# Attention and a softplus MLP on one core: the first stretch of all five engine queues written out as lists

## The chip, the cores and the metric

One of the eight cores of a Trainium2 chip. The core has five engines with a queue of their own, each strictly in order: TensorE (PE, matrix products), VectorE (DVE), ScalarE (ACT), GpSimd (POOL) and SyncE (SP, here the issuer of DMAs). Engines wait for each other through semaphores. The metric is the device time of one execution in microseconds, the median of several runs; lower is better.

## The reference

```python
q_d = q.reshape(B, H, Sd, factor, D).mean(axis=3)      # B, H, S, D = 4, 8, 576, 64; factor 4
...                                                    # k_d, v_d the same way
out_d = sm_attn(q_d, k_d, v_d)                         # softmax attention on 144 rows
out_up = np.repeat(out_d, factor, axis=2)
mask = np.abs(pos[:, None] - pos[None, :]) < factor
scores = np.where(mask, scale * np.matmul(q, k.transpose(0, 1, 3, 2)), -1000000000.0)
...                                                    # softmax of scores
out = out_up + np.matmul(attn, v)
x = out.transpose(0, 2, 1, 3).reshape(B * S, H * D)    # 2304 x 512
h = x @ w_in                                           # 512 x 2048
g = np.maximum(h, 0.0) + np.log1p(np.exp(-np.abs(h)))
return g @ w_out                                       # 2048 x 512
```

Inputs and outputs are float32.

## The kernel before

Attention runs in 16 units: unit u is one batch and one pair of heads (units 0 to 3 are batch 0). The MLP runs over 5 groups of 512 tokens (the last is shorter) and, within a group, over 16 tiles of 128 hidden features. A layer-1 tile h is 12 products of 128x512, a layer-2 tile adds 12 more into four accumulators acc. Each factor is split into a high part rounded to what TensorE reads (`fp32r`) and a low remainder, and three of the four products of parts are taken. The layer-1 input x of group 0 is batch 0's attention output, so the first layer-1 tiles need units 0 to 3.

One unit's steps, with the names that the lists of the change use for them (`name.unit`) and the engine that did them in batch 0 before:

- loads on SP: `q`, `k` (tiles qT, kT, already transposed), `vr` (v in rows, tile stage), `vw` (v in windows)
- `qd`, `kd`: sums of four neighbours (DVE); `block`: two scaled copies of qd (ACT); `vd`: the same sums of v, two additions (POOL)
- `psd`: downsampled scores (PE); `mxd` maximum (DVE), `expd` (ACT), `smd` reciprocal of the sum (DVE), `normd` (POOL); `pt0`, `pt1` transposes (PE, tile pdt), `sdT0`, `sdT1` copies (ACT)
- `psc`: local scores as 48 small products (PE), with the mask added by a product of the identity; `mx`, `sub` (DVE), `exp` (ACT), `sum`, `sm` (DVE), `norm` (POOL), `sT` transpose (DVE). Later units have the mask added on DVE (`mask`) in place of that product
- `po`: 4 + 48 products with vd and vw (PE), `od` (ACT), `x` two additions (DVE), `xh` rounded (ACT), `xl` remainder (POOL)

A weight block (`i` for layer 1, `o` for layer 2, `.f` for the tile) is loaded as 64-bit numbers and narrowed: `load` (SP), `top` (ACT), `or` (DVE), `hi` (ACT), `lo` (DVE). Layer-1 tile i: `l1_c.i` are the parts of its 12 products (tiles 0 to 2 in four quarters c of three products), then `abs`, `expln` (ACT), `max` (DVE), `gh` (POOL), `gl` (DVE), and `l2.i` the 12 products of layer 2. `fill_xh`, `fill_xl` are the part of batch 0 that belongs to group 1.

The order of all instructions is a planner's. `Plan.order` goes through time with a cost in microseconds for each operation: an engine that is free takes, of those whose inputs are ready and whose buffers can be had, the one of lowest priority number. Priorities are set by hand (batch 0's units start at `B0`, the others at `BS`). Delays are `LAT` = 0.2 between engines and `PE_LAT` = 0.8 or a `gap` in front of TensorE's steps; DMA runs at `DMA_RATE` = 0.33 MB/us with `DMA_LAT` = 2.0. `Plan.warm` then puts fillers into each gap that the plan has on TensorE ahead of layer 1: `busy(n)` issues n products of the identity with the mask (128x384) into a bank that nobody reads. A fixed 8 small ones (128x128) stand first:

```python
busy(8, identb)
for o in plan.warm(plan.order(), busy):
    o.fn()
```

The plan's order is what the engines get; the semaphores are added from the data that each instruction reads and writes.

Of the kernel before, what the change touches and what calls it, by code (L numbers as in the profile page):

```python
# [25 lines left out]
P = 128  # L26
# [27 lines left out]
TOP_POOL = lambda which, f: False  # L54
V_PE = ()
WL_POOL = lambda which, f: False
GL_ENG = lambda g: "DVE"
V_POOL = (0,)
NORM0 = "POOL"
O_POS = 4  # L60
NSPLIT = 3
BLOCK0 = "ACT"
KD_POOL = ()
XL_POOL = (0,)
# [39 lines left out]
class Plan:  # L104
    LAT = 0.2
    PE_LAT = 0.8
# [3 lines left out]
    DMA_LAT = 2.0  # L110
    DMA_RATE = 0.33
    AHEAD = 8
    def __init__(self, caps):
        self.caps, self.ops, self.state = caps, [], {}

    def op(self, eng, cost, prio, fn, r=(), w=(), after=(), kb=0.0, lat=None, block=False, port=False):
        o = Op(eng, cost, prio, fn)
        o.kb, o.block, o.port = kb, block, port or eng == "POOL"
        o.lat = lat if lat is not None else self.PE_LAT if eng == "PE" else self.LAT
# [22 lines left out]
    def order(self):  # L142
        waiting = {}
        line = {}
        for i, o in enumerate(self.ops):
# [8 lines left out]
        free = {e: 0.0 for e in waiting}  # L154
        port = 0.0
        frees = []
        dma_free, pos = 0.0, -50
# [3 lines left out]
        def ready_at(o):  # L161
            x = 0.0
            for d in o.deps:
                if d.end is None:
                    return None
                if d.eng == o.eng and d.eng != "SP":
                    x = max(x, d.end)
                else:
                    x = max(x, d.end + o.lat)
            return x  # L170

        while done < len(self.ops):
# [4 lines left out]
            for e, pend in waiting.items():  # L177
# [3 lines left out]
                for o in pend:  # L181
                    if o.prio > max(pos, 0 if e != "SP" else pos) + (self.AHEAD if pos >= 0 or e != "SP" else self.FETCH):
                        continue
# [15 lines left out]
                    if not turn:  # L199
# [41 lines left out]

    def warm(self, out, fill):
        last, extra = None, []
        for o in [x for x in out if x.eng == "PE"]:
            if last is not None:
                n = int((o.start - last) / self.FILL)
                if n > 1:
                    n += 2
                if n > 0:
                    x = Op("PE", 0.0, 0, lambda n=n: fill(n))  # L250
                    x.start = last
                    extra.append(x)
            if o.prio >= 0:
                break
            last = o.start + o.cost
        return sorted(out + extra, key=lambda o: o.start)
# [3 lines left out]
def kernel(  # L260
# [69 lines left out]
    def load(bf, src, prio, kb):  # L330
        return op("SP", 0.35, prio, lambda: nc.sync.dma_start(out=bf.t, in_=src), w=[bf], kb=kb)
# [3 lines left out]
    def attention(u, s):  # L335
# [3 lines left out]
        gap = 0.3 if early else 0.8  # L339
# [20 lines left out]
        if u in ON_PE:  # L360
# [11 lines left out]
            op("PE", 4.0, sS - 0.5, mm_sums, r=[q, k], w=[sums], lat=gap)  # L372
            qsum, qr = (lambda: sums.t[:, :SD]), [sums]
            op("ACT", 0.31, sS - 0.2, lambda: nc.scalar.copy(kd.t, sums.t[:, SD : 2 * SD]), r=[sums], w=[kd])
        else:
            qsum, qr = (lambda: qd.t), [qd]
            for dst, src, kk in ((qd, q, slice(0, S)), (kd, k, slice(REACH, REACH + S))):
                if src is k and u in KD_POOL:
                    ks = buf("ks", [P, 2, SD], 1, f"ks{u}", F32, first)

                    def pool_k(src=src, kk=kk, ks=ks):
                        v = src.t[:, kk].rearrange("c (s f) -> c f s", f=FACTOR)
                        nc.gpsimd.tensor_tensor(out=ks.t, in0=v[:, 0:2], in1=v[:, 2:4], op=ALU.add)
# [12 lines left out]
                    r=[src], w=[dst],  # L396
                )

        def copies():
            for j in range(2):  # L400
                hp = slice(j * D, (j + 1) * D)
                if be == "POOL":
                    nc.gpsimd.tensor_scalar(
                        out=bl[hp, j], in0=qsum()[hp], scalar1=scale, scalar2=None, op0=ALU.mult
                    )
                else:
                    nc.scalar.activation(out=bl[hp, j], in_=qsum()[hp], func=AF.Copy, scale=scale)

        be = BLOCK0 if early else "ACT"
        op(be, 0.66, sS - 1.5, copies, r=qr, w=[blk])  # L410
# [536 lines left out]
```

## Time and profile before

| what | us |
|---|---|
| median of 3 runs | 500.35 |
| lowest, highest | 500.2, 503.07 |
| profiled execution, its own time | 502.2 |
| profiled execution, span of the trace | 500.4 |
| TensorE busy in the span | 489.1 |
| VectorE busy | 269.3 |
| ScalarE busy | 245.0 |
| GpSimd busy | 92.6 |
| DMA, share of the 16 engines in queue q1 | 26.4% |

The profile is of one execution; the span lies between its first and its last recorded instruction. An engine's busy time is the union of its instructions' spans. Neighbours overlap a little, so the step from one row's start to the next row's start, and not a row's own duration, is what an instruction takes of its queue.

### The profile page before, as it was taken

How to read it: one execution, taken by the hardware profiler on the slowest of the kernel's cores; microseconds unless marked ns; L12 is line 12 of the kernel's file. 1: busy time of each engine (PE TensorE's matmuls, PEld its weight loads, DVE VectorE, ACT ScalarE, POOL GpSimd, SP SyncE). 2: the span in 40 equal slices, each digit the busy share in tenths (PEclk: the TensorE clock that was granted, in tenths of full speed). 3: DMA queues.
4: the chain of work that ended last, by engine and by line, in shares of the span. 5: the costliest groups of instructions: out<-in, count | busy, mean ns of one | idle time of the engine just before them, and what ended most of it. 6: DMA issues, size and time to landing. Idle time of an engine off the chain costs nothing.

```text
span 500.4 us, 12503 instructions
## 1 busy us (share of the span) xinstructions
PE 489.1 (98%) x5388; PEld 407.0 (81%) x5388; DVE 269.3 (54%) x512; ACT 245.0 (49%) x528; POOL 92.6 (19%) x133
## 2 busy tenths in 40 slices
PE   6999999999999999999999999999999999999996
PEld 4668778888878888888888888888888888889996
DVE  5668998898878646374274636453332222223322
ACT  3457988678656435434354535343442332334442
POOL 5633231131111121020011201120011001010110
PEclk9989999999999999999999999999999999999999
DMA  8924576666724303030114111100020000002001
GB/s 275 343 56 150 188 221 220 213 182 203 203 61 138 101 2 105 3 104 18 39 50 140 49 56 50 33 3 1 0 85 0 1 1 0 1 0 86 1 1 42
DMA packets 15798, 42.86 MB, mean 86 GB/s; under 512 B 1792, under 2 KB 2304, under 8 KB 15744
## 3 DMA queue, kind: packets, MB, share of 16 engines
q1 hardware_dynamic: 15600, 41.94, 26.4%
q8 instruction: 42, 0.69, 0.6%
q14 instruction: 12, 0.10, 0.1%
q10 hardware_dynamic: 144, 0.13, 0.1%
HBM read 37.35 MB, written 4.72 MB: 84 GB/s over the span
## 4 chain that ended last, share of the span: by engine, by line
PE 96%; DVE 1%; ACT 1%; DMA 1%; issue 0%
PE acc L809 40%; PE h L744 39%; PE po L593 5%; PE psc L492 3%; PE busy L900 3%; PE psd L429 3%; PE po L585 2%; PE pdt L561 2%; DMA qT<-in_qt_dram 1%; DVE qd L392 0%; DVE kd L392 0%; DVE wo0l L723 0%; PE psc L485 0%; DVE t L773 0%; DVE wri L698 0%
## 5 line engine op out<-in xcount | busy, mean ns | idle before, releaser
L773 DVE SCALAR_TENSOR_TENSOR t<-h,t 128x512 f32<-128x512 f32 (+1 forms) x80 | 50.7, 634 | 136.9 <-ACT t L768 136.9
L764 ACT ACTIVATE t<-h 128x512 f32<-128x512 f32 (+1 forms) x80 | 44.3, 554 | 156.7 <-PE h L744 151.9
L782 POOL TENSOR_SCALAR gh<-t 128x512 fp32r<-128x512 f32 (+1 forms) x80 | 51.6, 646 | 339.3 <-PE acc L809 152.4
L790 DVE TENSOR_TENSOR gl<-t,gh 128x512 fp32r<-128x512 f32 (+1 forms) x80 | 52.4, 655 | 40.7 <-POOL gh L782 40.7
L744 PE MATMUL h<-xh,wi0h 128*128 128x512 f32 (+1 forms) x160 | 60.7, 380 | 0.7 <-DVE t L773 0.7
L809 PE MATMUL acc<-gh,wo0h 128*128 128x512 f32 (+1 forms) x160 | 59.8, 374 | 0.0
L809 PE MATMUL acc<-gh,wo1h 128*128 128x512 f32 (+1 forms) x160 | 59.6, 373 | 0.0
L744 PE MATMUL h<-xh,wi1h 128*128 128x512 f32 (+1 forms) x160 | 59.5, 372 | 0.0
L809 PE MATMUL acc<-gl,wo1h 128*128 128x512 f32 (+1 forms) x160 | 59.1, 369 | 0.0
L744 PE MATMUL h<-xh,wi0l 128*128 128x512 f32 (+1 forms) x160 | 59.0, 369 | 0.0
L744 PE MATMUL h<-xl,wi0h 128*128 128x512 f32 (+1 forms) x160 | 59.0, 369 | 0.0
L809 PE MATMUL acc<-gl,wo0h 128*128 128x512 f32 (+1 forms) x160 | 58.9, 368 | 0.0
L744 PE MATMUL h<-xh,wi1l 128*128 128x512 f32 (+1 forms) x160 | 58.8, 368 | 0.0
L809 PE MATMUL acc<-gh,wo1l 128*128 128x512 f32 (+1 forms) x160 | 58.8, 368 | 0.0
L809 PE MATMUL acc<-gh,wo0l 128*128 128x512 f32 (+1 forms) x160 | 58.8, 368 | 0.0
L744 PE MATMUL h<-xl,wi1h 128*128 128x512 f32 (+1 forms) x160 | 58.8, 368 | 0.0
L768 ACT ACTIVATE t<-t 128x512 f32<-128x512 f32 (+1 forms) x80 | 47.2, 590 | 2.5
L767 ACT ACTIVATE t<-t 128x512 f32<-128x512 f32 (+1 forms) x80 | 47.2, 590 | 2.3
L744 PEld LDWEIGHTS h<-xh,wi0h 128*128 128x128 f32 x160 | 30.0, 188 | 6.3 <-DVE t L773 1.4
L744 PEld LDWEIGHTS h<-xh,wi0l 128*128 128x128 f32 x160 | 30.2, 189 | 5.6 <-DVE wi0l L723 0.3
L809 PEld LDWEIGHTS acc<-gl,wo1h 128*128 128x128 f32 x160 | 30.1, 188 | 5.3 <-DVE gl L790 0.5
L809 PEld LDWEIGHTS acc<-gh,wo0l 128*128 128x128 f32 x160 | 30.2, 189 | 5.1
(90 smaller groups left out, 767.2 us busy)
## 6 DMA issues: line engine op xcount, KB each, us to landing
wri<-in_w_in_dram SPq DMA_DIRECT2D x16, 511.8 KB, 4.7
wro<-in_w_out_dram SPq DMA_DIRECT2D x16, 511.8 KB, 4.3
vw<-in_vwin_dram SPq DMA_DIRECT2D x16, 384.0 KB
qT<-in_qt_dram SPq DMA_DIRECT2D x16, 292.0 KB, 3.1
kT<-in_kt_dram SPq DMA_DIRECT2D x16, 292.0 KB, 6.1
stage<-in_vrow_dram SPq DMA_DIRECT2D x16, 288.0 KB
out_dram<-osb SPq DMA_DIRECT2D x16, 256.0 KB, 2.8
out_dram<-osb SPq DMA_DIRECT2D x3, 128.0 KB, 1.8
```

The lines of the kernel that those rows point to most:

```text
L429: nc.tensor.matmul(pd3()[:, r, :], qb[:, r * RD : (r + 1) * RD], kd.t, start=True, stop=True)
L492: nc.tensor.matmul(pc()[o : o + HW, t, :], q.t[hp, c : c + HW], k.t[hp, c : c + HW], start=not early, stop=not early or t == NTL - 1,)
L593: nc.tensor.matmul(po[h].t[j * D : (j + 1) * D, t * HT : (t + 1) * HT], vw.t[kp, t, :], sT.t[kp, t, :HT], start=True, stop=True,)
L744: nc.tensor.matmul(h.t[:, :n], w[:, cc, fs], x.t[:, cc, cols(g)], start=(cc == 0 and k == 0), stop=(cc == NCC - 1 and k == 2),)
L764: op("ACT", c, pr, lambda: nc.scalar.activation(out=tv(), in_=hh(), func=AF.Abs), r=[h], w=[tt])
L767: nc.scalar.activation(out=tv(), in_=tv(), func=AF.Exp, scale=-1.0)
L768: nc.scalar.activation(out=tv(), in_=tv(), func=AF.Ln, bias=1.0)
L773: lambda: nc.vector.scalar_tensor_tensor(out=tv(), in0=hh(), scalar=0.0, in1=tv(), op0=ALU.max, op1=ALU.add),
L782: lambda: nc.gpsimd.tensor_scalar(out=gh.t[:, cols(g)], in0=tv(), scalar1=1.0, scalar2=0.0, op0=ALU.mult, op1=ALU.add),
L790: lambda: eng[ge].tensor_tensor(out=gl.t[:, cols(g)], in0=tv(), in1=gh.t[:, cols(g)].bitcast(F32), op=ALU.subtract),
L809: nc.tensor.matmul(acc[g][m].t[:, :n], w[:, f % FB, ms], a.t[:, cols(g)], start=(f == 0 and k == 0), stop=(f == NF - 1 and k == 2),)
L900: nc.tensor.matmul(h[:, :m], identb, wide, start=True, stop=True)
```

## The change

The order of the five engines is written out as five lists, from the start to the third layer-2 tile. While an engine's list lasts, the planner takes only its head; behind it, it chooses as before. `+3` in TensorE's list is three fillers; `Plan.warm` is gone. Of the lists the head and a few more entries of SP and PE:

```diff
+ORDER = {
+    "PE": """
+        +3 psd.0 psc.0 +2 psd.1 psc.1 +6 pt1.0 +2 pt0.0 +1 psc.2 psd.2 +2 psc.4 psd.3 pt1.1 +1 pt0.1
+        psc.3 +4 po.0 pt1.2 psd.4 pt0.2 po.1 +1 pt0.3 +2 pt1.3 +1 po.2 l1_0.1 l1_0.0 po.3 l1_1.1
+        l1_0.2 l1_1.0 l1_2.1 pt1.4 l1_3.1 l1_1.2 l1_2.0 l1_2.2 l1_3.0 pt0.4 l1_3.2 l1_0.3 l1_0.4
+        l2.0 l2.1 po.4 l1_0.5 l2.2
+    """,
...
+    "SP": """
+        k.0 q.0 q.1 iload.0 k.1 q.2 vr.1 vr.0 k.2 q.3 k.3 k.4 q.4 vr.4 vr.3 vr.2 vw.0 iload.1 vw.1
...
 class Plan:
-    LAT = 0.2
-    PE_LAT = 0.8
+    LAT = 0.035
+    TO_POOL = 0.08
+    DVE_TO_POOL = 0.18
+    PE_TAIL = 0.2
+    LAP = {"DVE": 0.08, "ACT": 0.1, "POOL": 0.04, "PE": 0.0, "SP": 0.0}
+    GAP = 0.8
...
-    DMA_LAT = 2.0
-    DMA_RATE = 0.33
+    DMA_START = 1.0
+    DMA_LAT = 0.6
+    DMA_RATE = 0.305
...
-                for o in pend:
-                    if o.prio > max(pos, 0 if e != "SP" else pos) + (self.AHEAD if pos >= 0 or e != "SP" else self.FETCH):
+                fixed = first.get(e)
+                for o in fixed[:1] if fixed else pend:
+                    if not fixed and o.prio > max(pos, 0 if e != "SP" else pos) + (self.AHEAD if pos >= 0 or e != "SP" else self.FETCH):
                         continue
...
         def mm_s():
-            if early:
-                nc.tensor.matmul(pc(), identb, mask, start=True, stop=False)
             for t in range(NTL):
...
+            if early:
+                nc.tensor.matmul(pc(), identb, mask, start=False, stop=True, skip_group_check=True)
...
-    nc.vector.tensor_copy(mask, base.unsqueeze(1).to_broadcast([P, NTL, HW]))
-    nc.vector.memset(mask[: P // 2, 0, :REACH], NEG)
-    nc.vector.memset(mask[P // 2 :, NTL - 1, HT + REACH :], NEG)
+    nc.gpsimd.tensor_copy(mask, base.unsqueeze(1).to_broadcast([P, NTL, HW]))
+    nc.gpsimd.memset(mask[: P // 2, 0, :REACH], NEG)
+    nc.gpsimd.memset(mask[P // 2 :, NTL - 1, HT + REACH :], NEG)
...
-    busy(8, identb)
-    for o in plan.warm(plan.order(), busy):
+    busy(24, identb)
+    for o in plan.order(busy):
         o.fn()
```

So the mask is made on GpSimd and its product stands last in a unit's scores, the small fillers at the start are 24, and the wide ones are the 25 that the list names, where the planner had put 64. A step may now run on another engine than its neighbours of the same kind: where a name stands in a list, that engine does it (`block.0` on DVE, `block.1` on POOL, `normd.1` on ACT, `od.0` on DVE, `ilo.0` on POOL). The costs of several steps and the planner's delays are other numbers, and they also rule the order behind the lists.

The queue of SP at its start, where stage is vr, wri a layer-1 weight block. Before:

```order
L331 DMA qT0_138<-in_qt_dram 128x584
L331 DMA kT0_140<-in_kt_dram 128x584
L331 DMA stage0_142<-in_vrow_dram 72x1024
L331 DMA vw0_144<-in_vwin_dram 128x768
L331 DMA qT1_146<-in_qt_dram 128x584
L331 DMA kT1_148<-in_kt_dram 128x584
L331 DMA stage1_150<-in_vrow_dram 72x1024
L331 DMA vw1_152<-in_vwin_dram 128x768
```

The same queue after the change:

```order
L406 DMA kT0_154<-in_kt_dram 128x584
L406 DMA qT0_156<-in_qt_dram 128x584
L406 DMA qT1_158<-in_qt_dram 128x584
L755 DMA wri0_160<-in_w_in_dram 128x2047
L406 DMA kT1_162<-in_kt_dram 128x584
L406 DMA qT2_164<-in_qt_dram 128x584
L406 DMA stage1_166<-in_vrow_dram 72x1024
L406 DMA stage0_170<-in_vrow_dram 72x1024
```

A unit's four loads stood together; now q and k of units 0 to 2 and the first weight block lead, and the windows of v come behind all of them.

The queue of POOL behind its memsets, where sd is what normd writes, sc what norm writes, and wi0l the remainder of a weight block. Before:

```order
L894 MEMSET top1_73 128x512
L414 TENSOR_TENSOR stage0_142<-stage0_142 72x4x128
L417 TENSOR_TENSOR vd0_223<-stage0_142 72x256
L414 TENSOR_TENSOR stage1_150<-stage1_150 72x4x128
L417 TENSOR_TENSOR vd1_318<-stage1_150 72x256
L471 TENSOR_TENSOR sd0_255<-sd0_255,smd0_332 96x432
L540 TENSOR_TENSOR sc0_233<-sc0_233,sm0_314 128x384
```

The same queue after the change:

```order
L973 MEMSET top1_73 128x512
L941 CAST mask_66<-base_89 128x384
L942 MEMSET mask_66 64x3
L943 MEMSET mask_66 64x5
L437 TENSOR_SCALAR block0_118<-qd1_188 64x144 x2
L540 TENSOR_TENSOR sd0_258<-sd0_258,smd0_271 96x432
L483 TENSOR_TENSOR stage1_166<-stage1_166 72x4x128
L486 TENSOR_TENSOR vd1_332<-stage1_166 72x256
L483 TENSOR_TENSOR stage0_170<-stage0_170 72x4x128
L486 TENSOR_TENSOR vd0_367<-stage0_170 72x256
L611 TENSOR_TENSOR sc0_327<-sc0_327,sm0_358 128x384
L801 TENSOR_TENSOR wi0l_76<-wri0_160,wi0h_75 128x4x128
```

The mask and block.1 now come first on GpSimd, the first unit's norm (sd) goes ahead of both sums of v, and a weight remainder is added.

The queue of DVE at the end of batch 0, up to the x of the last unit that layer 1 waits for. Before:

```order
L723 TENSOR_TENSOR wi0l_76<-wri0_309,wi0h_75 128x4x128
L613 TENSOR_TENSOR x0_579<-po2_0_753,od2_827 128x12x24
L613 TENSOR_TENSOR x0_579<-po2_1_748,od2_827 128x12x24
L698 SCALAR_TENSOR_TENSOR wri1_312<-wri1_312,top0_72 128x512
L698 SCALAR_TENSOR_TENSOR wro0_413<-wro0_413,top1_73 128x512
L440 TENSOR_REDUCE mxd4_897<-psd4_831 96x3
L723 TENSOR_TENSOR wi0l_76<-wri1_312,wi0h_75 128x4x128
L613 TENSOR_TENSOR x0_579<-po3_0_844,od3_905 128x12x24
L613 TENSOR_TENSOR x0_579<-po3_1_839,od3_905 128x12x24
```

The same place after the change:

```order
L619 STREAM_TRANSPOSE sT3_883<-sc3_694 128x384
L483 TENSOR_TENSOR stage3_252<-stage3_252 72x4x128
L486 TENSOR_TENSOR vd3_887<-stage3_252 72x256
L801 TENSOR_TENSOR wi0l_76<-wri2_445,wi0h_75 128x4x128
L776 SCALAR_TENSOR_TENSOR wri3_524<-wri3_524,top0_72 128x512
L686 TENSOR_TENSOR x0_799<-po2_0_829,od2_903 128x12x24
L686 TENSOR_TENSOR x0_799<-po2_1_824,od2_903 128x12x24
L587 TENSOR_REDUCE mx4_966<-sc4_530 128x12
L437 TENSOR_SCALAR od3_973<-po3_1_908 128x144
L686 TENSOR_TENSOR x0_799<-po3_0_913,od3_973 128x12x24
L686 TENSOR_TENSOR x0_799<-po3_1_908,od3_973 128x12x24
```

The sum of v of unit 3, its od and unit 4's maximum are now VectorE's, and the weight steps ahead of the last x have gone further along: the third remainder in place of the second.

## Rows read from the trace of the kernel before

**Rows 1.** The page: busy time by engine, and the chain that ended last by engine.

```profile
PE 489.1 (98%) x5388; PEld 407.0 (81%) x5388; DVE 269.3 (54%) x512; ACT 245.0 (49%) x528; POOL 92.6 (19%) x133
...
PE 96%; DVE 1%; ACT 1%; DMA 1%; issue 0%
```

**Rows 2.** Stretches: length, busy time of each engine (instructions), granted clock, DMA share, GB/s.

```profile
0.00:73.00 73.00, 65.67 (x1151) 50.31 (x1152) 54.94 (x112) 47.38 (x112) 29.72 (x47) 0.98 0.62 202
7.84:44.13 36.29, 34.45 (x830) 25.51 (x831) 25.23 (x59) 19.53 (x61) 17.23 (x18) 0.95 0.61 194
44.13:73.00 28.87, 28.20 (x217) 22.41 (x216) 26.82 (x47) 25.93 (x50) 7.20 (x7) 1.00 0.61 199
...
73.00:490.00 417.00, 416.89 (x4187) 350.48 (x4186) 211.91 (x395) 194.96 (x410) 62.08 (x84) 1.00 0.21 66
```

**Rows 3.** What TensorE waited for: total us, times, longest.

```profile
PE psc L485 <- DVE mask L864: 3.2, 1, 3.2
...
PE pdt L561 <- issue: 0.9, 1, 0.9
PE busy L900 <- issue: 0.8, 1, 0.8
PE h L744 <- DVE t L773: 0.7, 1, 0.7
```

**Rows 4.** Fillers alone from 0 to 43 us, then TensorE's timeline (start, us).

```profile
0.00:43.00 43.00, 15.80 (x72) 7.84 (x72) 0.96 0.63 207
...
1.64 1.03 PE L900 MATMUL busy<-identb 128*128 128x128 bf16 x8 [1.64 <-DVE identb L849]
5.86 0.48 PE L485 MATMUL psc<-mask,identb 128*128 128x384 bf16 x1 [3.18 <-DVE mask L864]
...
7.70 1.75 PE L429 MATMUL psd<-kd,block 128*96 128x144 f32 x6
9.25 3.52 PE L900 MATMUL busy<-mask,identb 128*128 128x384 bf16 x12
12.61 0.33 PE L485 MATMUL psc<-mask,identb 128*128 128x384 bf16 x1
...
13.82 1.31 PE L900 MATMUL busy<-mask,identb 128*128 128x384 bf16 x7
14.97 0.90 PE L429 MATMUL psd<-kd,block 128*96 128x144 f32 x6
15.70 1.14 PE L900 MATMUL busy<-mask,identb 128*128 128x384 bf16 x6
...
32.99 3.09 PE L900 MATMUL busy<-mask,identb 128*128 128x384 bf16 x9
```

**Rows 5.** The chain that ended last, behind the third layer-2 tile (start, us).

```profile
68.10 5.44 PE acc L809 x24
...
75.71 2.94 PE h L744 x12
```

**Rows 6.** Two neighbouring stretches, columns as in rows 2.

```profile
28.40:32.58 4.18, 3.97 (x207) 3.33 (x205) 3.46 (x10) 2.46 (x9) 1.85 (x3) 1.00 0.03 6
32.58:35.99 3.41, 3.41 (x15) 1.92 (x14) 3.41 (x8) 1.56 (x4) 0.83 (x1) 0.50 0.01 2
```

**Rows 7.** What VectorE waited for in the first 43 us, its largest entry.

```profile
DVE mxd L440 <- PE psd L429: 5.3, 4, 2.2
```

**Rows 8.** GpSimd's timeline: a memset, a product of 128x384, a remainder.

```profile
4.30 0.53 POOL L894 MEMSET top<- 128x512 int32 x1
...
28.51 0.83 POOL L540 TENSOR_TENSOR sc<-sc,sm 128x384 f32<-128x384 f32 x1
...
40.45 1.61 POOL L634 TENSOR_TENSOR xl<-x,xh 128x512 fp32r<-128x512 f32 x1 [1.81 <-ACT xh L628]
```

**Rows 9.** VectorE's timeline: two weight remainders.

```profile
41.36 1.25 DVE L723 TENSOR_TENSOR wi0l<-wri,wi0h 128x512 fp32r<-128x512 f32 x1
...
44.65 0.68 DVE L723 TENSOR_TENSOR wo0l<-wro,wo0h 128x512 fp32r<-128x512 f32 x1
```

More of the change, by code (lines that the diff above doesn't have):

```diff
@@ L53 @@
 ON_PE = ()
-TOP_POOL = lambda which, f: False
 V_PE = ()
[L56 to L59, printed above, removed]
 O_POS = 4
 NSPLIT = 3
-BLOCK0 = "ACT"
-KD_POOL = ()
-XL_POOL = (0,)
+HOME = {
+    "block": ("ACT", "ACT"),
+    "vd": ("POOL", "DVE"),
+    "normd": ("POOL", "DVE"),
+    "norm": ("POOL", "POOL"),
+    "sdT0": ("ACT", "ACT"),
+    "sdT1": ("ACT", "ACT"),
+    "od": ("ACT", "ACT"),
+    "xh": ("ACT", "ACT"),
+    "xl": ("POOL", "DVE"),
+    "itop": ("ACT", "ACT"),
+    "otop": ("ACT", "ACT"),
+    "ilo": ("DVE", "DVE"),
+    "olo": ("DVE", "DVE"),
+    "gl": ("DVE", "DVE"),
+}
@@ new lines @@
+COST = {
+    "block": {"ACT": 0.66, "DVE": 0.45, "POOL": 1.0},
+    "vd": {"POOL": 2.07, "DVE": 1.2},
+    "normd": {"ACT": 1.25, "DVE": 0.61, "POOL": 0.9},
+    "norm": {"DVE": 0.55, "POOL": 0.83},
+    "sdT0": {"ACT": 0.4, "DVE": 0.36},
+    "sdT1": {"ACT": 0.4, "DVE": 0.36},
+    "od": {"ACT": 0.29, "DVE": 0.25},
+    "xh": {"ACT": 0.6, "DVE": 0.65, "POOL": 0.85},
+    "xl": {"DVE": 0.7, "POOL": 1.27},
+    "itop": {"ACT": 0.75, "POOL": 0.95},
+    "otop": {"ACT": 0.75, "POOL": 0.95},
+    "ilo": {"DVE": 0.7, "POOL": 1.35},
+    "olo": {"DVE": 0.7, "POOL": 1.35},
+    "gl": {"DVE": 0.7, "POOL": 1.4},
+}
@@ L65, with home @@
+def home(name, i, later=True):
+    found = [e for e, names in ORDER.items() if f"{name}.{i}" in names.split()]
+    return found[0] if found else HOME[name][later]
 B0 = (-40, -32, -24, -16)
@@ L153, in order @@
         held = set()
-        free = {e: 0.0 for e in waiting}
+        free = {e: self.BEGIN.get(e, 0.0) for e in waiting}
         port = 0.0
         frees = []
-        dma_free, pos = 0.0, -50
+        dma_free, pos = 0.0, -70
         t, done, out = 0.0, 0, []
@@ L165, in ready_at @@
                     return None
[L166 to L169, printed above, removed]
+                x = max(x, d.end + self.hop(d.eng, o.eng) + (o.gap if d.eng != "PE" else 0.0))
             return x
@@ L198, in order @@
                         continue
-                    if not turn:
+                    if not turn and not fixed:
                         continue
@@ L208, in order @@
                     pos = max(pos, o.prio)
-                free[e] = o.end = t + o.cost
+                o.end = t + o.cost
+                free[e] = o.end - self.LAP[e]
                 if o.port:
@@ L240, in order @@
         return out
[L242 to L256, printed above, removed]
 @with_exitstack
@@ L401, in copies @@
                 hp = slice(j * D, (j + 1) * D)
[L402 to L410, printed above, removed]
+                copy_on(on("block"), bl[hp, j], qsum()[hp], scale)
+        e = on("block")
+        op(e, COST["block"][e], sS - 1.5, copies, r=qr, w=[blk], name="block")
         def pool_v():
-            e = nc.gpsimd if b in V_POOL else nc.vector
+            e = eng[on("vd")]
             e.tensor_tensor(
@@ L431, in mm_sd @@
                 )
-        op("PE", 0.75, sS + 0.5, mm_sd, r=[blk, kd], w=[psd], lat=gap, block=not early)
+        op("PE", 0.75, sS + 0.5, mm_sd, r=[blk, kd], w=[psd], lat=gap, block=not early, name="psd")
         mxd = buf("mxd", [RD, NR], 2, f"mxd{u}")
@@ L442, in attention @@
             ),
-            r=[psd], w=[mxd],
+            r=[psd], w=[mxd], name="mxd",
         )
@@ L451, in exps @@
                 )
-        op("ACT", 1.75, sT_ - 2, exps, r=[psd, mxd], w=[sd, ("smd2", u % 2)])
+        op("ACT", 1.2, sT_ - 2, exps, r=[psd, mxd], w=[sd, ("smd2", u % 2)], name="expd")
         def recip(x, pair):
@@ L457, in recip @@
             nc.vector.reciprocal(out=x.t, in_=x.t)
-        op("DVE", 0.35, sT_ - 1.2, lambda: recip(smd, smd2), r=[("smd2", u % 2)], w=[smd])
-        ne = NORM0 if early else "DVE"
+        op("DVE", 0.35, sT_ - 1.2, lambda: recip(smd, smd2), r=[("smd2", u % 2)], w=[smd], name="smd")
+        ne = on("normd")
         def norm_d():
@@ L512, in attention @@
                 ),
-                r=[psc], w=[sc],
+                r=[psc], w=[sc], name="mask",
             )
@@ L524, in attention @@
             ),
-            r=rd + [mx], w=[sc], port=not early,
+            r=rd + [mx], w=[sc], port=not early, name="sub",
         )
@@ L672, in weight, with op @@
         prio = 2 * f - 2 if which == "i" else 2 * f + O_POS
+        def op(e, cost, prio, fn, name, **kw):
+            name = (which + name, f)
+            return plan.op(e, cost, prio, fn, name=name, **kw)
         st = buf("stage", [P, DM, 4], 4, f"wr{which}{f}", U16)
```

205 lines of the change are left out of this document (127 added, 78 removed).

## The prediction

> **What bounds the kernel now.** The page first [rows 1]: TensorE is busy for 98% of the span and the chain that ended last is 96% TensorE, so the time is the length of TensorE's queue, and only what stands in that queue without need, or keeps it waiting, can go. Then the table by stretches [rows 2]: from 73 us to 490 us TensorE is idle for 417.00 - 416.89 = 0.1 us. An order cannot gain anything there. In the first 73 us it is idle for 73.00 - 65.67 = 7.33 us, and some of its busy time is filler (`busy`, products that nobody reads). The waits [rows 3] name the idle time: 1.64 us for the identity at the start [rows 4], 3.2 us for the mask, two waits of 0.9 and 0.8 us with no releaser ("issue"), and 0.7 us for VectorE. The fillers [rows 4]: 72 of them, 15.80 us busy. Each of the nine wide groups overlaps the next row by about 0.16 us (9.25 + 3.52 = 12.77, while the next row starts at 12.61) and the 8 small ones take 1.03, so the wide ones hold the queue for 15.80 - 1.03 - 9 x 0.16 = 13.3 us. All that time other engines were working towards what TensorE would need next, but with pauses: VectorE stood idle for 36.29 - 25.23 = 11.1 us between the first maximum and the last x [rows 2], half of it for products psd that stood behind fillers [rows 7].
>
> **The common work.** Take as set S what TensorE has done in the new lists when the third layer-2 tile ends: the attention of units 0 to 4, layer-1 tiles 0 to 5, layer-2 tiles 0 to 2. Before, S and one layer-2 tile more are done at 75.71 us, and two such tiles take 5.44 us [rows 5]; so S alone is 75.71 - 2.72 = 72.99 us. Behind S both kernels go on with the same work, at a TensorE without gaps, so the change in time is the change in the end of S, plus what waits appear behind it.
>
> **What the change makes of it, part by part.** S holds 72.99 - 7.33 - 1.03 - 13.3 = 51.3 us of work that stays. Two pieces of it ran at the low clock. The first scores and downsampled scores took 9.25 - 5.86 = 3.39 us, the second unit's (13.82 - 12.61) + (15.70 - 14.97) = 1.94 us [rows 4]: 1.45 us too much. And from 32.58 to 35.99 us the granted clock was 0.50 [rows 6]; nine fillers filled most of it, so about 0.3 us of real work was stretched. Warm work: 49.5 us.
>
> When it begins. The first two loads are now k and q of unit 0 in place of q and k, equal in size, so the first landings stay. The mask has moved from VectorE to GpSimd, behind the last memset that ends at 4.83 us [rows 8]. A GpSimd copy of 128x384 is in no row; it lies between that memset (0.53) and the longest of these rows (1.61), and the nearest, a product of the same 128x384, took 0.83 us [rows 8]; I take that. With two small memsets the mask stands at about 5.9 us, three wide fillers wait for it (0.3 us each at the low clock, as 12 took 3.36 us [rows 4]), and psd.0 starts at 6.8 us. That is later than the old first product (5.86), and VectorE, free of the mask, has the reductions and the block copy done by then.
>
> Low clock at the start: 24 small fillers now run from 1.64 us. They may bring the clock up before psd.0 (0) or not (1.45 us); I take the middle, 0.7. Fillers behind psd.0: 22 by 0.164 us (7 took 14.97 - 13.82 = 1.15 [rows 4]), 3.6 us. So with no wait at all S would end at 6.8 + 49.5 + 0.7 + 3.6 = 60.6 us.
>
> Waits that I add. The two issue waits of 1.7 us [rows 3] belong to a stretch of the trace with dense small products, which stays: 1.7, between 0 and 3.4, since the dense products now follow each other faster. Data that comes too late: see the next paragraph; I take two waits of the size of VectorE's one [rows 3], 1.4 us, between 0 and 9.7. A drop of the clock: before it fell when a stretch with no wide filler in it had passed, although TensorE was busy for 3.97 of its 4.18 us [rows 6]. The new list has four fillers from po.0 to po.3, where the old order has 24, so I expect a drop of that length once: 3.41 us at half speed cost half of it, 1.7 us (0 to 5, three drops). The sum: 60.6 + 1.7 + 1.4 + 1.7 = 65.4 us, 7.6 us before the old 72.99.
>
> [...]
>
> **Is the data there in time?** Fillers and waits were TensorE's slack for VectorE, so VectorE's own queue must be added up. From mxd.0 to the last x it holds 65 instructions where 58 stood from mx.0 to the last x (it gains vd.3, ilo.2, ior.2, ior.3, two od and unit 4's smd, mask and mx; it gives ilo.0 and ilo.1 to GpSimd, and qd.1 and oor.0 move out of the stretch). The window's 59 were busy 25.23 us, 0.43 us each [rows 2]; seven more make 28.2 us. psd.0, which took 1.75 us at the low clock [rows 4], ends at about 8.5 us, so x.3 comes at 36.7 us if VectorE never stops, and with its rounding on ScalarE and the remainder on VectorE (0.65 each; a remainder took 0.68 [rows 9]) the last quarter of the layer-1 input stands at 38.0 us. TensorE gets to the first product that reads it when S still lacks 7.5 tiles of 2.72 us, unit 4's po (75.71 - 73.54 = 2.17 us [rows 5]) and a transpose, 22.9 us together: at 60.6 - 22.9 + 1.7 = 39.4 us. Room: 1.4 us. Behind it 30 VectorE instructions of 26.82 / 47 = 0.57 us [rows 2] stand before gl.2, which is then there at 53.8 us, 5.8 us ahead of its use at 59.6 us; ScalarE is 90% busy there [rows 2] and eats into that. So VectorE, no longer TensorE's fillers, is what S hangs on at 38 us, and any further delay there goes straight to the end.
>
> GpSimd gets the mask, one block copy, and three of the weight remainders. Where such a remainder on VectorE ran beside GpSimd's, it took 1.25 us in place of 0.68 [rows 9], and GpSimd's 1.61 [rows 8]: 0.57 us on VectorE each time. Four VectorE instructions of two inputs (ior.1 to ior.3, ilo.2) now stand beside a full GpSimd: at most 2.3 us, 0.9 more than the room, which lies within the 1.4 us above. [...]
>
> The loads: v's rows now come behind q and k of all five units, and the window of v (vw) behind them. Nothing but vd and po reads them, and the scores of five units, with their reductions and exponentials, lie ahead of po.0 to hide them; I cost that at nothing. If the cover fails, TensorE stops at po.0, behind which psd.4, the transposes of units 2 and 3 and all of layer 1 are queued: each microsecond of lateness then costs one. The new delay constants also order everything behind the lists; 0.1 us of idle time in 417 leaves no gain, and I take no loss.
>
> **The rivals.** Forecast: the median of 500.35 us less 7.6 is 492.8 us. (The profiled execution took 502.2 us with a span of 500.4; its own time would fall to 494.6.)
> First rival, VectorE as the bound: its queue keeps half of the 11.1 us of pauses, since each of its steps waits for TensorE or ScalarE in turn. Then the last quarter stands at 43.5 us, TensorE waits 4.1 us there in place of 0.7, and the time is 496.2 us. For it: the chain mxd, exponential, sum, norm, transpose crosses four engines. Against it: q and k of all units are there early, and other units' steps stand between.
> Second rival, ending slower: the clock is low from po.0 to po.3. The products of that stretch (four po of 2.17 us [rows 5], one psd of 0.73, four half transposes of about 0.28, two quarters of a layer-1 tile of 0.68) come to some 12 us and would take 24. The drop already charged falls away: 492.8 + 12 - 1.7 = 503.1 us. If it reaches back over the scores of units 2 to 4 (three of 1.21 with psd of 0.73, 6 us), it is 509 us. It decides once the low clock has lasted 2 x (7.6 + 1.7) = 18.6 us of wall time. For it: four fillers in place of 24. Against it: one drop only before, and six full-size products of layer 1 now stand between po.2 and po.3.
> Third rival, better: neither issue waits nor drop: 492.8 - 3.4 = 489.4 us.
> That the lists are not what the chip gets is no rival: the built program has them engine by engine.
>
> **How the numbers follow.** Forecast 0.56, VectorE as the bound 0.24, better 0.10, low clock 0.06, anything else 0.04. About 1% (5 us) is what a measurement can tell from no change. Over 1% faster: the forecast, the better case and a quarter of the first rival, 0.72; slower by over 1%: the longer half of the low clock and a little, 0.04; the rest 0.24. The range runs from the better case, 489.4, to 498.0, where VectorE would pause two thirds of what it did.
>
> **What would show it.** In the changed profile: psd.0 at 6.8 us; the last x on VectorE at about 37 us (before 43.3 to 44.1); the third layer-2 tile ending at 65 us; VectorE over 85% busy from 9 to 37 us; TensorE idle under 4 us behind 7 us; at most one short stretch of low clock. I am wrong if TensorE waits for VectorE or ScalarE by more than 4 us before S ends, or behind S, where the weights of the next tiles come later than the earlier products need them.

## The result, and the profile after

Changed kernel 502.96 us (21 runs), before 499.97 us (21 runs): ratio 1.006, 95% interval 1.0039 to 1.008. The forecast was 492.8 us; the time lies outside its range, on the other side of no change: slower by 0.6%. Ratios leave out executions over 1.5% above the fastest of their kernel, medians do not; the one profiled with the result was such (512.85 us), so the rows here are, where nothing else is said, those of the same kernel run again in the first experiment (own time 508.28 us, span 506.5 us).

Its page, busy time and chain, against [rows 1]:

```profile
PE 490.9 (97%) x5365; PEld 411.2 (81%) x5365; DVE 265.7 (52%) x511; ACT 245.9 (49%) x530; POOL 88.7 (18%) x138
...
PE 91%; ACT 2%; issue 2%; DMA 2%; DVE 1%; SPq 0%; ACTq 0%
```

TensorE is busy for 1.8 us more than before, though 39 wide fillers are gone (25 in place of 64): some of its work ran slower. The stretches, columns as in [rows 2]; the third layer-2 tile, the end of S, ends at 79.2 us:

```profile
7.00:16.64 9.64, 6.74 (x216) 5.16 (x216) 5.86 (x12) 3.02 (x10) 5.40 (x7) 1.00 0.99 297
16.64:20.06 3.42, 3.42 (x107) 2.53 (x106) 2.84 (x7) 2.87 (x11) 2.33 (x3) 0.50 1.04 271
20.06:23.47 3.41, 0.37 (x2) 0.25 (x2) 1.26 (x4) 1.66 (x5) 1.71 (x2) 1.00 1.01 309
23.47:30.30 6.83, 5.37 (x112) 4.54 (x112) 2.30 (x5) 1.19 (x6) 0.00 (x0) 0.50 0.84 336
30.30:37.12 6.82, 5.92 (x220) 4.76 (x219) 5.34 (x16) 5.05 (x17) 4.95 (x5) 1.00 0.03 10
37.12:50.78 13.66, 13.66 (x231) 10.56 (x231) 8.83 (x21) 9.23 (x24) 6.01 (x5) 0.50 0.35 124
...
79.20:496.00 416.80, 416.14 (x4089) 350.14 (x4089) 210.00 (x395) 196.10 (x412) 56.32 (x85) 1.00 0.20 63
```

Behind S little has changed (0.66 us idle in 416.8, where [rows 2] had 0.11 in 417). Ahead of it stand three stretches at a granted clock of 0.50, 23.9 us together; [rows 6] had one of 3.41. TensorE's waits, against [rows 3]:

```profile
PE psd L498 <- issue: 4.5, 1, 4.5
PE psc L559 <- issue: 2.7, 1, 2.7
PE busy L979 <- DVE identb L928: 1.7, 1, 1.7
PE busy L979 <- POOL mask L943: 1.5, 1, 1.5
PE po L665 <- issue: 0.8, 1, 0.8
PE psd L498 <- DVE x L686: 0.7, 1, 0.7
PE psd L498 <- DVE kd L466: 0.2, 1, 0.2
```

Issue waits are 8.0 us in place of 1.7 ([rows 3] leaves out a third, of 0.2 us), waits for VectorE behind the start 0.9 us. TensorE's timeline where they stand:

```profile
6.76 1.65 PE L498 MATMUL psd<-kd,block 128*96 128x144 f32 x6
...
11.48 0.92 PE L559 MATMUL psc<-kT,qT 64*32 64x32 f32 x84
15.14 0.32 PE L559 MATMUL psc<-kT,qT 64*32 64x32 f32 x12 [2.73 <-issue]
...
18.48 1.51 PE L559 MATMUL psc<-kT,qT 64*32 64x32 f32 x96
...
20.14 0.29 PE L498 MATMUL psd<-kd,block 128*96 128x144 f32 x1
24.93 1.36 PE L498 MATMUL psd<-kd,block 128*96 128x144 f32 x5 [4.50 <-issue]
...
33.49 0.65 PE L665 MATMUL po<-sT,vw 32*64 32x24 f32 x30
34.96 1.22 PE L665 MATMUL po<-sT,vw 32*64 32x24 f32 x66 [0.82 <-issue]
```

It stops in the midst of a group of equal products whose inputs are all there: after 84 of 96, after one of six, after 30 of 96. What ends the stop is in the profile's queue of instructions, 42 packets of 16 KB in the span (0.69 MB); the result's profile has as many, for the 10806 instructions of TensorE's queue there, 257 to a packet. They are called pages of code here. From 22.3 to 23.6 us, ahead of the second resumption, while the loads (q1) took 96.3% of the same 16 engines:

```profile
q8 instruction: 1, 0.02, 5.2%
```

Counted one by one in the trace, TensorE's queue had begun 449 instructions at the first stop, 705 at the second and 1217 at the third: 256 apart, and twice 256. (Products and weight loads alone are 444 and 697 at the first two; nearly all the rest are semaphore instructions.) The page that landed last ahead of each resumption, from the packets:

```
                page lands   TensorE goes on   instruction
run again          13.88          15.14            449
                   23.52          24.93            705
                   33.38          34.96           1217
result's profile   13.03          14.27            449
                   22.98          24.34            705
before             19.41          20.66            705 (stop of 0.9)
```

VectorE, which was to be the bound, waits for TensorE, and the last x comes at 53.4 us:

```profile
DVE mxd L509 <- PE psd L498: 7.6, 4, 4.7
DVE mx L587 <- PE psc L568: 3.8, 2, 2.9
...
53.38 0.82 DVE L686 TENSOR_TENSOR x<-po,od 128x288 f32<-128x288 f32 x2
```

### The profile page after: what moved, and what is told of

It is laid out like the page before. It is cut to its first block, busy times and chain, and to the rows that moved or that the text cites. A ratio compares the mean times of both kernels' runs of the same rounds, so it can differ in the third digit from the quotient of the medians.

```text
span 511.1 us, 12456 instructions
## 1 busy us (share of the span) xinstructions
PE 493.8 (97%) x5365; PEld 413.4 (81%) x5365; DVE 265.7 (52%) x511; ACT 245.3 (48%) x530; POOL 88.3 (17%) x138
## 4 chain that ended last, share of the span: by engine, by line
PE 91%; ACT 2%; DMA 2%; issue 2%; DVE 1%; SPq 0%; ACTq 0%
PE h L822 38%; PE acc L888 38%; PE po L665 5%; PE psc L559 3%; PE psd L498 3%; PE po L657 2%; PE pdt L632 2%; DMA wri<-in_w_in_dram 1%; DMA wro<-in_w_out_dram 1%; PE busy L979 1%; ACT top L769 1%; ACT t L847 0%; ACT t L846 0%; ACT t L843 0%; DVE wri L776 0%
## 5 line engine op out<-in xcount | busy, mean ns | idle before, releaser
L869 DVE TENSOR_TENSOR gl<-t,gh 128x512 fp32r<-128x512 f32 (+1 forms) x80 | 50.7, 633 | 41.9 <-POOL gh L861 41.8
L822 PE MATMUL h<-xh,wi0h 128*128 128x512 f32 (+1 forms) x160 | 61.9, 387 | 0.0
L822 PE MATMUL h<-xl,wi0h 128*128 128x512 f32 (+1 forms) x160 | 60.3, 377 | 0.0
L822 PE MATMUL h<-xh,wi0l 128*128 128x512 f32 (+1 forms) x160 | 60.2, 376 | 0.0
L822 PEld LDWEIGHTS h<-xl,wi0h 128*128 128x128 f32 x160 | 30.9, 193 | 4.9
```

The lines of the kernel that those rows point to most:

```text
L822: nc.tensor.matmul(h.t[:, :n], w[:, cc, fs], x.t[:, cc, cols(g)], start=(cc == 0 and k == 0), stop=(cc == NCC - 1 and k == 2),)
L869: lambda: eng[ge].tensor_tensor(out=gl.t[:, cols(g)], in0=tv(), in1=gh.t[:, cols(g)].bitcast(F32), op=ALU.subtract),
```

## The experiments

Theories: A, TensorE waits for pages of code, which wait behind the loads on the same 16 DMA engines (A2: pages are too slow for such dense products even without the loads). B, the low clock that follows from stops and few fillers. C, the order itself: waits between engines. The instructions 444 and 697 of the expectations are 449 and 705 of the table, counted without semaphore instructions.

**The changed kernel again.** No edit.

> The changed kernel as it is, for a profile of an undisturbed execution. Theory A (code): TensorE stops because its next page of instructions is not there; the pages travel on the same 16 DMA engines as the loads. Then the issue waits come to 5 us or more here too, each stop ends 1 to 1.5 us behind the end of a page in the queue of instructions, and the time is 501 to 504 us. Theory B (clock): the stops are short here, and the loss is low clock alone: granted clock 0.99, about 10 us at the low level, where the kernel before has 0.996. Theory C (order): the waits of TensorE for VectorE, ScalarE and GpSimd come to more than 4 us behind 7 us.

503.25 us (501.25 to 513.84), ratio 1.006 (1.0022 to 1.0098); rows above. A held (8.0 us, the stops ending 1.3, 1.4 and 1.6 us behind a page). Of B, the executions of this kernel in both sets show the price: those at a granted clock of 0.99 took some 502.8 us, those at 0.966 some 513.5: 10.7 us for an estimated 24 us more at the low clock (0.024 x 2 x 507, its level taken as the 0.50 of the rows), 0.44 us each. Three between 0.973 and 0.98 took some 507.8 us: 5.0 us for 14 us more, estimated the same way, 0.35 each. C failed (0.9 us).

**Loads held back.** The window of v of unit 0, and all loads queued behind it, wait for a one-element memset on VectorE.

```diff
+        if u == 0:
+            plan.op("DVE", 0.1, 0, lambda: nc.vector.memset(vw.t[0:1, 0, 0:1], 0.0), w=[vw], name=("gate", u))
-        ... qd.3 kd.2 kd.3 mx.2 smd.1 sT.0 ...
+        ... qd.3 kd.2 kd.3 mx.2 gate.0 smd.1 sT.0 ...
```

> The window of v of unit 0, and with it all loads behind it in SP's queue, may start only when VectorE has taken unit 2's maximum. A: the DMA engines run empty before, TensorE's second page of code lands by 19 us, the long stop (4.6 us in the changed kernel's profile) falls under 1.5 us, the time is 497 to 499.5 us. B: the low clock decides; the time stays within 1 us of the changed kernel unless the clock's share changes. C: nothing is won, and po.0 comes later by the lateness of the windows, up to 3 us: 503 to 506 us.

508.03 us, 1.0159 (1.0128 to 1.0189). TensorE's issue waits:

```profile
PE psc L561 <- issue: 5.2, 2, 3.6
PE po L667 <- issue: 1.7, 1, 1.7
...
PE psd L500 <- issue: 0.7, 1, 0.7
```

The wait in psd fell from 4.5 to 0.7 us as A says: SP issued nothing from 14.6 to 21.9 us, and the second page started at 19.45 us, when 4.81 of the 4.99 MB issued by 14.6 us had landed; it started 3.4 us after the first stop's end, where it took 7.3 us without the gate (15.14 to 22.43). But the first page came later in this execution (14.80), the next two stops (instructions 961 and 1217) cost 1.6 and 1.7 us, and with 7.6 us of issue waits left and a clock of 0.976 the sum got worse. Of A the long stop held; its page, wanted by 19 us, landed at 20.74, and its time failed.

**More fillers late.**

```diff
-        psc.3 +4 po.0 pt1.2 psd.4 pt0.2 po.1 +1 pt0.3 +2 pt1.3 +1 po.2 l1_0.1 ...
+        psc.3 +8 po.0 +4 pt1.2 psd.4 pt0.2 +8 po.1 +4 pt0.3 +4 pt1.3 +4 po.2 l1_0.1 ...
```

> 24 more wide fillers (8, 8 or 4 ahead of po.0 to po.2, of psd.4 and of the late transposes), 0.164 us each at full clock, 3.9 us together. B: the clock stays up from 30 us on, clock 0.995 and better, the time does not rise, 499 to 503 us, and the executions of 507 to 514 us go away. A: the stops at 12 and 20 us are ahead of the new fillers and stay; the fillers cost what of them isn't hidden, 503 to 507 us. C: as A.

504.98 us, 1.0108 (1.0082 to 1.0133), four executions within 504.8 to 506.1. The third low stretch is gone:

```profile
24.44:27.86 3.42, 3.08 (x94) 2.37 (x97) 1.07 (x2) 0.99 (x5) 0.00 (x0) 0.50 0.96 392
27.86:75.83 47.97, 46.97 (x822) 37.43 (x810) 39.56 (x80) 36.95 (x83) 17.59 (x16) 1.00 0.48 160
```

So few fillers were the cause of that stretch, as B says; the clock was 0.988 to 0.996 in all four. The stops stayed (9.0 us of issue waits), and the fillers cost what the clock gave: A's time.

**The kernel before without fillers, with a third, with two thirds.** `plan.order()` in place of `plan.warm(plan.order(), busy)`; and `fill(n // 3)` (19 fillers) or `fill(n * 2 // 3)` (40) in `warm`, where 64 stood.

> The kernel before without its 64 wide fillers, which hold 13.3 us of TensorE's queue; nothing else moves. A: TensorE comes to the end of its code pages sooner, with the same loads in the DMA queues: issue waits rise from 1.8 us to 5 us or more, and little of the 13.3 us is won: 497 to 503 us. B: the clock is low for 10 us or more in the first 45 us and takes the gain back. C: the issue waits stay near 1.8 us, and what is lost stands as waits for VectorE and ScalarE.

> The kernel before with two thirds of the wide fillers of each group (40 in place of 64, 3.9 us of queue less). B (the clock takes back what fewer fillers give): time within 1.5 us of before, with the clock lower, 0.985 to 0.995. If the old groups are larger than the clock and the code pages need: clock still 0.997 or better, 496 to 498 us, faster than both kernels.

> The same with one third (19 in place of 64, 7.4 us of queue less). B: clock 0.975 to 0.985, 501 to 504 us, between before and the run without fillers (504.8). If the groups are too large: 494 to 497 us.

| wide fillers | us, median | ratio, 95% interval | clock of the profile |
|---|---|---|---|
| 64 (before, five sets of runs) | 499.2 to 500.6 | | 0.996 |
| 40 | 500.4 | 1.0041 (1.0002 to 1.0081) | 0.993 |
| 19 | 504.3 | 1.0099 (1.0065 to 1.0132) | 0.976 |
| 0 | 504.8 | 1.0078 (1.0052 to 1.0104) | 0.973 |

Each ratio is against the kernel before in the same set of runs (499.2 us for 40 and 19, 500.6 for 0).

Long low stretches without fillers:

```profile
16.98:27.22 10.24, 10.14 (x221) 8.68 (x221) 6.43 (x15) 5.76 (x20) 6.15 (x6) 0.50 0.91 324
...
30.63:47.70 17.07, 16.92 (x343) 13.88 (x336) 9.62 (x18) 10.95 (x27) 5.00 (x4) 0.50 0.22 66
```

With 19:

```profile
28.65:49.13 20.48, 19.53 (x387) 16.11 (x387) 10.31 (x21) 11.41 (x28) 5.49 (x5) 0.50 0.17 55
```

B held in the old order too: up to 13.3 us of queue taken out, and nothing won. A, which wanted 5 us of issue waits without fillers, failed here (1.1 us). Perhaps TensorE, at the low clock, came to its page ends late enough; no run tested that.

**Fewer loads.** This kernel computes something else: units 1 to 3 use q, k and windows of unit 0, as the expectation says, and the second weight block waits at a gate (not in the cut). Without and with the late fillers.

```diff
+        if 0 < u < NPAIR:
+            q, k = one[:2]      # likewise vw = one[2]
-        k.0 q.0 q.1 iload.0 k.1 q.2 vr.1 vr.0 k.2 q.3 k.3 k.4 q.4 vr.4 vr.3 vr.2 vw.0 iload.1 vw.1
-        iload.2 iload.3 vw.2 oload.0 vw.3 iload.4 ...
+        k.0 q.0 iload.0 vr.1 vr.0 k.4 q.4 vr.4 vr.3 vr.2 vw.0 iload.1
+        iload.2 iload.3 oload.0 iload.4 ...
```

> Units 1 to 3 compute with q, k and the windows of v of unit 0, whose loads are left out (2.9 MB of the 8.7 MB of the first 30 us), and the weight blocks behind the first wait for unit 2's maximum. The lists of the four computing engines stay. A (code pages behind loads): the first page lands by 10.5 us, the second within 4 us of the moment its stop asks for it, issue waits fall from 7 to 8 us to under 2.5 us, and the time to 495 to 499 us. A2 (code pages are too slow by themselves for such dense products, loads or not): the stops behind instructions 444 and 697 stay at over 5 us together, the time within 2 us of the changed kernel's 503. C (order): neither; the waits for other engines fill the place, 501 to 504 us.

> As the run before, with the 24 more wide fillers of the fill run (3.9 us of queue). If A and B (clock) are the whole loss: issue waits under 2.5 us, low clock under 5 us behind 7 us, the third layer-2 tile ends at 67 to 71 us in place of 75.8 us with the fillers alone, and the time is 494 to 498 us. If C has a part: over 499 us, with waits of TensorE for VectorE or ScalarE of more than 3 us.

Without fillers 503.39 us, from 496.5 to 507.8; the ratio, 0.9992 (0.9958 to 1.0027), is of five of the ten executions. With them 501.44 us, 1.0029 (1.0 to 1.0058), 498.1 to 504.9. A profile of the first (own time 497.05 us, one of the two best of the ten):

```profile
PE psc L567 <- issue: 2.3, 1, 2.3
PE psd L506 <- issue: 1.8, 1, 1.8
...
7.00:24.72 17.72, 13.52 (x449) 10.20 (x449) 13.58 (x33) 11.40 (x43) 11.18 (x12) 1.00 0.76 235
24.72:28.13 3.41, 3.29 (x91) 2.10 (x92) 1.40 (x5) 1.60 (x4) 0.72 (x1) 0.50 0.06 20
28.13:67.00 38.87, 38.87 (x656) 32.00 (x654) 33.11 (x65) 31.07 (x63) 14.70 (x13) 1.00 0.53 176
```

The second page lands at 17.27 us in place of 23.52, the issue waits are halved (4.1 us; A wanted under 2.5, so A2 has a part), the last x comes at 41.4 us and S ends at 67.1 us, near the forecast's 65.4. The others spread with the clock (507.8 us at 0.972, 496.5 at 0.996). C has little part here: behind the start TensorE waits 1.5 us for VectorE, and where code and clock let it, the order comes near what it was counted for. With the late fillers the issue waits fell to 2.0 us, as expected, but the clock was low for 6.83 us, S ended at 72.0 us, and the forecast of 494 to 498 us failed; the waits for VectorE and ScalarE, 1.6 us, are not C's 3.

**Shallower queue.** Six gates like the one above (k.1, k.2, k.4, vw.0, vw.2, vw.3), the weight blocks behind the first three windows; with and without the late fillers.

> All loads stay, but six of them (k.1, k.2, k.4, vw.0, vw.2, vw.3) and what is queued behind them on SP may start only when VectorE has come to a set place, so that some 1 MB is queued in place of 1.5 to 2.3 MB; the weight blocks go behind the windows. A: a page of code waits for less: the first lands by 11.5 us in place of 12.6 to 14.4, the second by 19 us in place of 22 to 23.5, issue waits 2 to 4 us, time 497 to 501 us. A2: stops as before, 503 us or more. C: the later loads hold TensorE up instead, 503 to 507 us.

> The run before with the 24 more wide fillers. A and B together: issue waits 2 to 4 us, clock 0.995 or better, 496 to 500 us, the best of the kernels that compute everything. B alone or A2: 503 to 506 us, as the fill run. C: over 503 us with waits for loads or VectorE.

509.93 us, 1.0209 (1.015 to 1.0267); with fillers 506.49, 1.0119 (1.0081 to 1.0156). Pages came sooner as A says (11.84 and 18.94 us in place of 13.88 and 23.52), but issue waits were 6.4 us (6.8 with fillers) where A wanted 2 to 4; TensorE reached the second page's end sooner too (17.4 us in place of 20.1) and waited there again. The clock was low for 23.9 us (mean 0.976), as in the run again. The times failed.

**Two parts alone, in the kernel before.** First its start (mask on GpSimd, its product last, 24 small fillers: the diff's lines); then its loads.

```diff
-        load(q, qt[u], s - 9 if early else s - 1, 292)
+        load(q, qt[u], u - 60 if early else s - 1, 292)
...
-        load(vr, vrow[u], s - 3 if early else s + 4, 288)
+        load(vr, vrow[u], u - 56 if early else s + 4, 288)
```

> The kernel before with one part of the change, its start: the mask made on GpSimd, its product last in a unit's scores, 24 small fillers in place of 8. A and B: the first scores no longer wait for the mask (3.2 us before) and run at the higher clock, all fillers of the planner stay and with them the pace of the code pages: issue waits within 1 us of before, clock as before, 1.5 to 3 us faster, 497 to 498.5 us. C: the planner's order behind it was made for the old start, and VectorE or ScalarE are late instead: within 1 us of before.

> The kernel before with one part of the change, the order of loads: q and k of units 0 to 3 lead, then the rows and windows of v. The planner then puts the scores of units 1 to 3 nearly one behind the other (one wide filler between them, where 12 and 13 stood) and po.0 later. A (code pages behind loads, dense products): TensorE comes to its page ends sooner and stops there, issue waits over 5 us, 501 to 505 us, clock at or under 0.99. C (no code limit): the earlier scores give VectorE its work sooner, 495 to 499 us, issue waits near 2 us.

The start: 501.54 us, 1.0018 (0.9988 to 1.0048): nothing, where A and B wanted 1.5 to 3 us. The scores begin 1.6 us sooner, but their last product waits for the mask:

```profile
4.69 1.28 PE L490 MATMUL psc<-kT,qT 64*32 64x32 f32 x96 [0.29 <-DMA kT<-in_kt_dram]
8.56 0.32 PE L499 MATMUL psc<-mask,identb 128*128 128x384 bf16 x1 [2.59 <-POOL mask L865]
```

The loads: 507.23 us, 1.0146 (1.0104 to 1.0188), issue waits in four places:

```profile
PE psc L492 <- issue: 2.0, 2, 1.1
PE po L593 <- issue: 1.4, 1, 1.4
...
PE pdt L561 <- issue: 1.0, 1, 1.0
```

The load order, with what the planner made of the rest behind it, cost more than the whole change. Issue waits of 4.4 us are less than A's 5, and 1.0 us of them (pdt) is not at a page's end; the second page lands about as before (18.92 us, before 19.41), and the clock is 0.992. So only part of its 7 us has a name.

**Fillers where TensorE stood still.** 43 of them; then 12 more behind.

```diff
-        +3 psd.0 psc.0 +2 psd.1 psc.1 +6 pt1.0 +2 pt0.0 +1 psc.2 psd.2 +2 psc.4 ...
+        +3 psd.0 psc.0 +12 psd.1 +8 psc.1 +10 pt1.0 +2 pt0.0 +14 psc.2 +8 psd.2 +2 psc.4 ...
```

> The changed kernel with 43 more wide fillers (7.1 us at full clock) ahead of psd.1, psc.1, the first transpose, psc.2 and psd.2, where TensorE stood idle for 7 to 9 us in the profile of the changed kernel run again (7.4 us of code stops, 1.7 us for kd.1). A and B: they stand in idle time, so they cost under 2 us, the stops shrink to under 3 us together, and the clock does not drop behind them until 28 us: 499 to 502 us. If the stops are not of a pace of code (253 instructions in some 6 us) but come wherever these instructions stand, they stay, and the fillers cost their 7 us: 507 to 510 us.

> The run before with 12 fillers more (2.0 us) from po.0 to po.2, half of those of the fill run. A and B: clock 0.997 or better, 497 to 500.5 us, at least as good as the kernel before. B overrated: the fillers only cost, 2 us over the run before.

505.71 us, 1.0117 (1.0072 to 1.0162), and 506.65, 1.0137 (1.0104 to 1.017). In the first one's profile there is no low stretch at all (1.00 from 7 to 78 us), and it is still no faster:

```profile
7.00:78.00 71.00, 61.26 (x1240) 48.08 (x1240) 50.94 (x107) 46.33 (x113) 27.07 (x27) 1.00 0.63 209
...
PE psc L559 <- issue: 5.7, 3, 3.0
...
PE psc L568 <- issue: 1.4, 1, 1.4
PE po L665 <- issue: 0.2, 1, 0.2
```

The fillers moved other work to the ends of the pages, but the stops again begin at instructions 449, 705, 961 and 1217. The one at 705 ends at 24.1 us, not much sooner than without the fillers (24.9): the second page lands at 22.79 us, and the fillers themselves are 86 of the instructions that pages bring. Both ranges failed; the fillers were not free, the stops at 449 and 705 shrank (2.7 to 0.6 us, 4.5 to 3.0), and the two behind them grew. One execution had a mean granted clock of 0.95 and took 505.44 us, which the price above doesn't fit; it has no profile.

**Gate and fillers together.** Both edits.

> The changed kernel with the gate on the windows of v (second page lands by 21 us) and the 43 wide fillers ahead of the page ends (clock at 1.0). A and B as two separate losses of the changed order: issue waits under 5 us, clock 0.995 or better, 498 to 502 us, that is under both of the runs with one of the two (508.0 and 505.7 us). If they are one loss that only changes its place: 504 to 508 us.

513.28 us, 1.0232 (1.016 to 1.0303). Issue waits are down to 4.2 us, and behind them:

```profile
7.00:32.59 25.59, 21.34 (x588) 15.58 (x588) 14.64 (x35) 13.24 (x46) 12.25 (x14) 1.00 0.79 258
32.59:59.90 27.31, 27.31 (x454) 22.26 (x451) 15.59 (x38) 12.13 (x29) 9.47 (x8) 0.50 0.25 85
```

That is above both expectations. The two losses do not add up separately: with half of the issue waits gone the clock was low for 27.31 us. No kernel here that computes everything beats the one before.

## Why the prediction was wrong

By its own terms, for the profile above: 65.4 + (8.0 - 1.7) issue waits + (9.2 - 1.7) clock + (1.3 - 0.7) at the start + (0.9 - 1.4) data = 79.3 us; S ended at 79.2 (its last tile starts at 76.45 and takes 2.72). The clock's 9.2 is an estimate: TensorE was busy for 3.42 + 5.37 + 13.66 = 22.45 us in the low stretches; po.1 took 3.86 us there and po.3 2.19 at the high clock, a unit's scores 1.44 and 0.95, so some 1.7 times as long, and 22.45 x (1 - 1 / 1.7) = 9.2. By the scores alone it would be 7.6, so the sum's agreement to 0.1 us is in part luck. Of po.1 and po.3 the first row and the row behind, and the third layer-2 tile:

```profile
37.75 1.23 PE L657 MATMUL po<-sdT,vd 72*64 72x144 f32 x8
...
41.61 0.50 PE L979 MATMUL busy<-mask,identb 128*128 128x384 bf16 x1
...
50.68 0.74 PE L657 MATMUL po<-sdT,vd 72*64 72x144 f32 x8
...
52.87 0.50 PE L822 MATMUL h<-xh,wi0h 128*128 128x512 f32 x1
...
76.45 0.39 PE L888 MATMUL acc<-gh,wo0h 128*128 128x512 f32 x1
```

The 1.3 is psd.0 and psc.0, 1.58 + 1.44 us against 0.73 and 0.95. That the low clock made them long is the author's estimate from their lengths, as in the prediction, and not shown; the profile gives 1.00 there. In the result's profile, behind the same 24 small fillers, they took 0.83 + 0.95 us: the forecast's 0 to 1.45 is what the executions span.

```profile
6.31 0.90 PE L498 MATMUL psd<-kd,block 128*96 128x144 f32 x6
7.14 1.02 PE L559 MATMUL psc<-kT,qT 64*32 64x32 f32 x96
```

- **What bounds the kernel; psd.0 at 6.8 us; waits for data**: right (6.76 us; 0.9 us in place of 1.4).
- **Issue waits**, the first step that failed: sized by the old waits, 1.7 us and twice that at most, and measured at 8.0. They are no share of dense work but an arrival: a page for each 256 instructions, as the counts at the stops show (449, 705, 1217), and the second landed 8.4 us after TensorE had gone on from the first stop (15.14 to 23.52). A unit's scores are 192 instructions (96 products, 96 weight loads) in 1 to 1.5 us; the old fillers, two instructions in 0.16 us, had let time pass at little code. (That is argued, and one run speaks against it as the whole reason: the old kernel without fillers waited only 1.1 us.) The "loads at nothing" belong here: the second page landed at 23.5 in place of 19.4 us, and fewer loads or a gate moved it to 17.3 or 20.7, so that loads delay it is shown. That the new order of the loads made it later than before is not: with q and k put ahead in the old kernel it landed at 18.92. Nor is it shown that a page waits for all that was issued ahead of it. By bytes it nearly comes out in the run with the gate (above) and in the run again (5.89 MB landed when the page started, 5.91 issued by 15.5 us), but with the loads alone the page started at 17.82 us, when 4.83 MB had landed of the 5.90 issued by 13.04 us, where TensorE had gone on. The prediction also misread the new list: the rows of v of units 1 and 0 stand ahead of k.2, not behind q and k of all five units.
- **Drop of the clock**, the second: 1.7 us (0 to 5) for what was an estimated 10 us at the low level in most executions (from their clock of 0.99, at 0.50) and 23.9 in the profile; at 0.35 to 0.44 us each some 3.5 to 4.4, inside its range, and, by the estimate above, 9 us, outside it. The removed fillers (9.7 us net) were the forecast's gain, and the runs with 40, 19 and 0 fillers show that the old order gained nothing from fewer either.
- **VectorE's ledger**: not reached, since TensorE was late; VectorE was busy for 16.34 of the 28 us from 9 to 37 us, 58% in place of 85%. The first rival did not come.
- **Second rival** (chance 0.06): its mechanism came, with the low clock from po.1 up to po.3 in this profile, and its 503.1 us is close to the median by luck: it charged 12 us to the clock, where most executions paid some 4 and the code cost the rest. The trace of before had its sign, a drop behind a stretch that was 95% busy [rows 6]; "one drop only before" read the effect of 64 fillers as a property of the work.

For the median: 492.8 + 6.3 of code + 1.8 to 2.7 of clock (3.5 to 4.4, less 1.7) = 500.9 to 501.8 us, measured 502.96. The 6.3 is from an execution at 0.975 (the result's own profile, at 0.965, has 7.7 us of issue waits); no execution at 0.99 was profiled.

What stays open: why some executions of one kernel have 10 us at the low clock and others 24, what of the load order's 7 us is neither code nor clock, and how much a page takes when no loads are in its way: the third stop, 0.8 us, came with the DMA engines 3% busy (30.30 to 37.12 us), which speaks for a part of A2.

## What to carry to other kernels

Products that nobody reads can hold the clock up: from 64 to 0 of them in the old order it went from 0.996 to 0.973. That they also buy time for the next page of code is not shown: 43 of them shortened two stops and lengthened two. Before taking fillers out, run the kernel without them; here that run would have warned against this forecast. A stop in the midst of a group of equal instructions whose inputs are there was code here (three of them, 8.0 us, each ending 1.3 to 1.6 us behind a page): count all instructions of the queue up to it, look for the page that landed just ahead, and at what was issued to the DMA queues before. Where two limits are coupled, as code and clock were here, time bought back from one can go to the other: with gate and fillers together the issue waits fell from 8.0 to 4.2 us, and 27.31 us passed at 0.50 in place of 23.9.

## What the runs showed of the hardware

Code pages cost TensorE 8.0 us within 30 us, at instructions 449, 705 and 1217; where variants of the new order stopped for code, it was at these or at 961, also with 43 fillers moving other work there. At the first two stops, 7.2 us, the 16 DMA engines were 99% and 101% busy (the rows 7.00:16.64 and 20.06:23.47), at the third, 0.8 us, 3%.

The granted clock stayed at 0.50 for 27.31 us in which TensorE was busy without a gap (the run with gate and fillers together, 32.59:59.90), with full 128x512 products of layer 1 in it, 0.43 us from one to the next, where behind it, at 1.00, they took 0.23; the absence of gaps did not raise it in that time.
